# Four VectorE passes instead of five to decode float64 weights, a second slot for magnitudes, and local values in 64-row tiles

## The chip, the cores and the metric

One NeuronCore of a Trainium2 chip runs the whole program. The metric is the device time of one execution in microseconds (us). Three runs of the kernel before took 944.45 to 945.38 us, median 944.99.

## The reference

Three stages follow one another, all in float32 results:

- Attention on q, k, v of shape (4, 8, 576, 64). Two outputs are added: a pooled one (q, k, v averaged in groups of four tokens, softmax over 144 positions, repeated four times) and a local one (each token sees only tokens less than four away, softmax, times v). The heads are laid side by side to x with 2304 tokens of 512.
- A gated layer: `(x @ w_a) * (x @ w_b) @ w_out`, with 512 to 1536 to 512.
- A second layer: `h = x @ w_in; (h * clip(h + 3, 0, 6) / 6) @ w_out`, with 512 to 2048 to 512.

The weights arrive as float64. What the kernel must do with them before any matmul is to turn 64-bit words into 32-bit ones.

## The kernel before, in words

**Precision.** Large matmuls take each operand as two float32r parts (a rounded value and the rest) and three passes (line 635 for the first layer, 692 for its output, 818 and 943/958 for the second layer, whose 2x2 blocks are combined by a seven-product scheme).

**Decoding.** `decode` (line 239) makes a float32 from each float64, 1024 of them on each of 128 partitions, that is one weight tile: 34 tiles in all (12 `wab`, 6 `wo`, 8 `w2i`, 8 `w2o`). A tile is loaded as 8 bytes per weight (line 247) and seen as two uint32 views with a step of two words, `lo` and `hi`. The steps are:

- `magnitude`, ScalarE (256): absolute value of `hi` read as float32, into the tile `m` of tag "dm", of which there is one.
- `exponent`, VectorE (262, 263): clamp, shift left by 3 and mask, in place in `m`.
- `upper`, VectorE (267): the top bits of `hi` joined with `m`, written to `hi`.
- `lower`, VectorE (273, 274): the power of two of the result into `m`; `lo` times 2^-52 times that.
- `both`, VectorE (280): `hi` + `lo`, written to `hi`.
- For `wab` and `wo` then `first` (ScalarE, 284, the rounded part) and `second` (VectorE, 287, the rest); `w2i` and `w2o` have their own steps behind `both`.

**Attention.** Twenty local units of up to 116 tokens (`local`, line 503) and sixteen pooled groups (`pooled`, 375). In a local unit, two sub-blocks of 58 tokens each look at 64 keys. The probabilities of the two heads of a pair lie after the transpose on partitions 0 to 63 and 64 to 127 of `eT`. The values tile `vz` holds the two heads likewise, with a half of zeros for each, so that the product (line 576) takes all 128 rows of `eT` and writes 64 columns of one PSUM bank, `po`. The zeros are written once by GpSimd (line 348), the values by two DMAs per unit (line 517). The score products (line 529) use tiles of 64 rows and 64 columns, in all four positions, with one PSUM bank for each row half.

**Order.** No engine's order is written by hand. `Plan` (line 57) is a list scheduler: every step has an engine, an estimated duration, a due time `want`, predecessors, and slots that it takes and gives. It plays the steps through in estimated time and issues, on each engine, the ready step that is due first; that fixes the order of each engine's in-order queue, SyncE's DMAs included. So any change of estimates, slots or predecessors gives a new order on every engine. Until the first block of x is ready, a filler (line 186, tile `unread`) puts matmuls of no use on TensorE wherever the plan leaves it idle; `end_fill` ends that.

The first layer's jobs (`job`, 618) begin as soon as x of the first block (units 0 and 1) and `wab` tile 0 are there; attention of later units and the decoding of the other `wab` tiles run beside them, to about 300 us. Then come `wo` and `w2i`, the first layer's output (437 to 580 us) beside the decoding of `w2o`, and the second layer (581 us to the end).

Of the kernel before, what the change touches and what calls it, by code (L numbers as in the profile page):

```python
# [9 lines left out]
F32 = mybir.dt.float32  # L10
F32R = mybir.dt.float32r
BF16 = mybir.dt.bfloat16
U32 = mybir.dt.uint32
AF = mybir.ActivationFunctionType
ALU = mybir.AluOpType
# [3 lines left out]
P = 128  # L19
D = 64  # L20
# [3 lines left out]
KB = 64  # L24
QB = KB - 2 * HALO
# [4 lines left out]
HP = 4  # L30
# [2 lines left out]
XT = 3 * UT  # L33
NC = 512
FILL = 0.4
NB = 384
CUT = 4
BANK = 512
# [108 lines left out]
def fused_kernel(ctx: ExitStack, tc: tile.TileContext, qk, vt, vd, wab, wo, w2i, w2o, mask, out):  # L147
    nc = tc.nc
# [3 lines left out]
    F1 = wab.shape[0]  # L152
    F2 = 2 * w2i.shape[0]
    W = 2 * DM
# [5 lines left out]
    dp = dctx.enter_context(tc.tile_pool(name="dec", bufs=1))  # L160
# [4 lines left out]
    ap = actx.enter_context(tc.tile_pool(name="attn", bufs=1))  # L165
# [17 lines left out]
    def fill():  # L183
        if not unread:
# [4 lines left out]

    plan = Plan()  # L190

    BUFS = {"wh": F1, "raw": 2, "dm": 1, "qk": 4, "vraw": 1, "dqk": 2, "de": 2, "dv": 3, "deT": 2, "od": 2, "e": 2,
            "eT": 2, "xf": 2, "x": 4, "a": 2, "b": 4, "s2": 2, "wo": F1 // 2, "w2": 2, "hg0": 3,
            "hg1": 1, "xo": 3, "q": 8, "ws": 2, "x0": 4, "L": 24, "c": 14}
    plan.cap.update(BUFS)
# [4 lines left out]
    def slot(pool, shape, dtype, tag, name):  # L200
        return pool.tile(shape, dtype, tag=tag, bufs=BUFS[tag], name=name)


    def dve(n):
        return 0.07 + 0.00106 * n

    def dve2(n):
        return 0.1 + 0.00055 * n

    def act(n):  # L210
        return 0.1 + 0.00095 * n
# [9 lines left out]
    def ACT(busy, want, run, after=(), take=(), give=(), slack=0.0):  # L221
        return plan.add("ACT", busy, want, run, after, take, give, ACT_L + slack)

    def DVE(busy, want, run, after=(), take=(), give=(), slack=0.0):
        return plan.add("DVE", busy, want, run, after, take, give, DVE_L + slack)
# [10 lines left out]
    wab_t, wo_t, w2_t = {}, {}, {}  # L236
    pools = {}

    def decode(src, want, put, tag, after=(), ahead=4, slack=1.0, raw=None, step=CUT):

        T = {}

        def load(a, b):
            def run():
                if a == 0:
                    T["raw"] = slot(xp if raw == "x" else dp, [P, CUT, W // CUT], mybir.dt.uint64, raw or "raw", "raw")
                nc.sync.dma_start(T["raw"][:, a:b], src[a:b].rearrange("a p c -> p a c"))
            return run

        def words():  # L250
            w = T["raw"].rearrange("p a c -> p (a c)").bitcast(U32).rearrange("p (n t) -> p n t", t=2)
            return w[:, :, 0], w[:, :, 1]

        def magnitude():
            T["m"] = slot(dp, [P, W], F32, "dm", "m")
            nc.scalar.activation(T["m"], words()[1].bitcast(F32), AF.Abs)  # L256

        def exponent():
            m = T["m"]
            mu = m.bitcast(U32)  # L260

            nc.vector.tensor_scalar(m, m, W_MIN, W_MAX, op0=ALU.max, op1=ALU.min)
            nc.vector.tensor_scalar(mu, mu, 3, 0x3FFFFFF8, op0=ALU.logical_shift_left, op1=ALU.bitwise_and)

        def upper():
            hi = words()[1]
            nc.vector.scalar_tensor_tensor(out=hi, in0=hi, scalar=0xC0000000, in1=T["m"].bitcast(U32),
                                           op0=ALU.bitwise_and, op1=ALU.bitwise_or)

        def lower():  # L270
            m, (lo, hi) = T["m"], words()

            nc.vector.tensor_scalar(m.bitcast(U32), hi, 0xFF800000, None, op0=ALU.bitwise_and)
            nc.vector.scalar_tensor_tensor(out=lo.bitcast(F32), in0=lo, scalar=2.0 ** -52, in1=m,  # L274
                                           op0=ALU.mult, op1=ALU.mult)

        def both():
            lo, hi = words()
            v = hi.bitcast(F32)
            nc.vector.tensor_tensor(v, v, lo.bitcast(F32), op=ALU.add)  # L280

        def first():
            T["w"] = put()
            nc.scalar.activation(T["w"][:, 0], words()[1].bitcast(F32), AF.Copy)

        def second():
            nc.vector.tensor_tensor(T["w"][:, 1], words()[1].bitcast(F32), T["w"][:, 0], op=ALU.subtract)


        i, loads = None, []  # L290
        for a in range(0, CUT, step):
            i = DMA(256 * step, want - ahead, load(a, a + step), [i and issued[i]], take=[] if a else [raw or "raw"])
            loads.append(i)
        i = loads
        i = ACT(act(W), want, magnitude, i, take=["dm"], slack=slack)
        i = DVE(2 * dve2(W), want, exponent, [i])
        i = DVE(dve(W), want, upper, [i])
        i = DVE(dve2(W) + dve(W), want, lower, [i], give=["dm"])
        if put is None:
            return DVE(dve(W), want, both, [i], slack=slack), words  # L300
        i = DVE(dve(W), want, both, [i], slack=slack)
        i = ACT(act(W), want, first, [i, *after], take=[tag], slack=slack)
        return DVE(dve(W), want, second, [i], give=[raw or "raw"])

# [37 lines left out]
        return plan.add("-", 0, want, lambda: None, ends, give=[raw or "raw"])  # L342


    vz = [ap.tile([P, 2, 2, HP, D], F32, name=f"vz{i}") for i in range(2)]
    for t in vz:
        for h in range(2):
            nc.gpsimd.memset(t[64 - 64 * h:128 - 64 * h, h], 0.0)

    def unit_tokens(u):  # L350
        return min(UT, S - u % NU * UT)
# [1 line left out]
    place, sizes = {}, []  # L353
    for m, n in enumerate(BLOCKS):
        sizes.append(0)
        for _ in range(n):
            u = len(place)
# [6 lines left out]
    S_ = {}  # L364
# [8 lines left out]
    def one_bank(name):  # L373
        return slot(ps, [P, BANK], F32, "b", name)
# [131 lines left out]
    def local(u, want, soon):  # L506

        L = {}
        b, j = divmod(u, NU)
        tokens = unit_tokens(u)  # L510
        m, at = place[u]
        v_ = vz[u % len(vz)]

        def load():
            for h in range(2):
                r = slice(64 * h, 64 * h + 64)
                nc.sync.dma_start(v_[r, h], vt[u, r])

        def score():
            sc = L["sc"] = two_banks("sc")  # L520
# [47 lines left out]
        def pv():  # L568
            po_ = one_bank("po")
            L["po"] = po_[:, :HP * UT].rearrange("d (p t) -> d p t", p=HP)  # L570
            if soon:
                nc.tensor.matmul(L["po"].rearrange("p a (s r) -> p a s r", r=FACTOR), ident, pooled_part(), start=True, stop=False)
            for p in range(HP):
                for i in range(2):
                    for h in range(2):
                        nc.tensor.matmul(L["po"][64 * h:64 * h + 64, p, i * QB:(i + 1) * QB], v_[:, h, i, p],  # L576
                                         L["eT"][:, p, i * KB:i * KB + QB], start=not soon,
                                         stop=(not soon or (p == HP - 1 and i == 1)))
            if soon:
                L["xf"] = L["po"]  # L580
# [18 lines left out]
        def x_second():  # L599
# [5 lines left out]
        i = PE(0.9, want, score, [S_["sums" if last else "qk", b, g] for g in range(HP)], take=["s2"],  # L605
               give=["qk" if b else "wh"] * HP if last else [])
        S_["score", u] = i
        i = DVE(dve(n) + 0.2, want, top, [i], give=[])
        for p in range(HP):
            i = ACT(2 * 0.31, want, exps(p), [i], take=[] if p else ["e"], give=["s2"] if p == HP - 1 else [])  # L610
        i = DVE(0.36, want, inverse, [i])
        i = DVE(dve(n), want, norm, [i])
        i = PE(0.5, want, turn, [i], take=["b", "turn", "eT"], give=["e"])
        i = ACT(act(n), want, turned, [i], give=["b", "turn"])
        ods_ = [S_["od", b, g] for g in range(HP)]
        i = S_["pv", u] = PE(1.7 if soon else 0.9, want, pv, [i, ld] + ods_,
                             take=["b", "pv"] + ([] if soon else ["xf"]), give=["eT"])
        if not soon:
            i = DVE(dve(n), want, total, [i], give=["b", "pv"] + (["od"] if last else []))
        i = ACT(act(n), want, x_first, [i, S_.get(("x", u - 1)) if at else None], take=[] if at else ["x"])  # L620
# [405 lines left out]
    for u in place:  # L1026
        m = place[u][0]
        i = (place[u][1] + UT - 1) // UT
        t = when[m, 0] - 4 + 0.1 * i if m < 3 else T1 - 30 + 4 * i if m == 3 else T1 - 14 + 1.25 * (i + 3 * m - 12)
# [8 lines left out]
    i = plan.add("PE", 0.01, -1000, fill, take=["b", "m"])  # L1038
    plan.add("-", 0, -1000, end_fill, [i, *(S_["x", u] for u in place if place[u][0] < 1)], give=["b", "m"])
    for f in range(F1):  # L1040
        S_["wab", f] = decode(wab[f], when[0, f] - 4, lambda f=f: wab_t.setdefault(f, slot(wpool, [P, 2, W], F32R, "wh", "wh")),
                              "wh", ahead=26 if f < 2 else 6, slack=0.0)
    for t, (n, f) in enumerate(jobs):
        job(n, f, t, n == NBLK - 1)

# [17 lines left out]
        pctx.close()  # L1063
        pools["ps"] = ctx.enter_context(tc.tile_pool(name="ps2", bufs=1, space=PSUM, reuse_waits="tile"))

    S_["p2"] = plan.add("-", 0, 0, open_p2, [S_["x2", u] for u in place])
    S_["ps"] = plan.add("-", 0, 0, open_ps, [S_["both", n, f] for n, f in jobs[-2:]])

    for i in range(F1 // 2):
# [91 lines left out]
    for i, (n, h) in enumerate((n, h) for n in ORDER for h in range(2)):  # L1161
# [8 lines left out]
        def second(n=n, h=h):  # L1170
# [3 lines left out]
        j = DMA(512, T4 - 24 + 4 * i, load, [x for k in range(CUT * h, CUT * h + CUT) for x in S_["w_d", k]],  # L1174
                take=["wh" if i < F1 else "w2"])
        j = ACT(act(W), T4 - 4 + 4 * i, first, [j])
# [74 lines left out]
```

## Time and profile before

| what | value |
|---|---|
| median of three runs | 944.99 us (944.45 to 945.38) |
| span of the profiled execution, first to last instruction | 942.6 us |
| granted TensorE clock, mean | 1.000 |
| TensorE busy | 934.3 us, 99% |
| VectorE busy | 756.3 us, 80% |
| ScalarE busy | 457.8 us, 49% |
| GpSimd busy | 5.2 us, 1% |
| q1 (the DMA queue of loads and stores) | 49.5% of 16 engines' span |

The profiled execution's own time is not listed apart from its span; the span lies 2.4 us below the median of the runs, and that difference is used for what lies around it. Busy time counts an engine as at work from an instruction's start to its modelled end; the ends of matmuls overlap, so a busy TensorE can still lose time between starts. The page's second part shows the share by 40 slices, the chain of work shows what released what, and the windows view gives busy time by stretch.

### The profile page before, as it was taken

To read this page: it belongs to the slowest core of one execution; us is meant where nothing else is said; L and a number is where in the kernel's file an instruction comes from. 1 tells how busy PE (TensorE), PEld (TensorE's weight loads), DVE (VectorE), ACT (ScalarE), POOL (GpSimd) and SP (SyncE) were. 2 spreads that over 40 slices of the span, in tenths; PEclk is the share of its full clock that TensorE was granted. 3 is DMA by queue.
4 is the path that set the end of the run, shared out by engine and by line. 5 is a ranking of instruction groups with operands and counts; after the bars stand their busy time and mean duration, and the time that the engine had idled before them with its cause. 6 is when DMAs were issued, how large, how long until landed. Compare 5 with 4: busy or idle time off the path is not lost.

```text
span 942.6 us, 19148 instructions
## 1 busy us (share of the span) xinstructions
PE 934.3 (99%) x7306; PEld 874.4 (93%) x7306; DVE 756.3 (80%) x1376; ACT 457.8 (49%) x1164; POOL 5.2 (1%) x44
## 2 busy tenths in 40 slices
PE   9999999999999999999999999999999999999998
PEld 6678999999889999998888889999999999999998
DVE  4999989824736969586877766999898999897983
ACT  3867534535555324223445445545455574554551
POOL 1000000000000000000000000000000000000000
PEclk9999999999999999999999999999999999999999
DMA  9544763423304444426678887425247881806401
GB/s 273 190 125 139 224 218 120 154 70 120 96 31 137 172 149 135 135 81 196 195 227 246 260 264 230 151 97 190 101 164 259 269 259 52 279 7 206 131 18 51
DMA packets 103789, 151.26 MB, mean 160 GB/s; under 512 B 8848, under 2 KB 72336, under 8 KB 103696
## 3 DMA queue, kind: packets, MB, share of 16 engines
q1 hardware_dynamic: 102976, 148.80, 49.5%
q8 instruction: 57, 0.93, 0.4%
q10 hardware_dynamic: 720, 1.23, 0.4%
q14 instruction: 36, 0.29, 0.1%
HBM read 100.19 MB, written 49.81 MB: 159 GB/s over the span
## 4 chain that ended last, share of the span: by engine, by line
PE 92%; DVE 5%; ACT 1%; DMA 1%; issue 1%; DVEq 0%; ACTq 0%
PE pab L635 33%; PE ph L818 19%; PE oacc L958 15%; PE acc L692 14%; PE po L576 2%; PE dsc L426 2%; PE dpo L476 1%; PE sc L529 1%; DVE in L748 1%; PE pt L562 1%; PE oacc L943 1%; PE unread L186 1%; PE dpt L458 1%; ACT e L546 1%; DVE e L914 1%; DMA h<-h_d 1%
## 5 line engine op out<-in xcount | busy, mean ns | idle before, releaser
L635 PE MATMUL pab<-x,wh 128*128 128x344 f32 (+2 forms) x2016 | 321.9, 317 | 0.4 <-DVE x L600 0.4
L635 PEld LDWEIGHTS pab<-x,wh 128*128 128x128 f32 x2016 | 306.2, 188 | 4.3 <-issue 2.0
L818 PE MATMUL ph<-in,w 128*128 128x384 f32 x1008 | 175.3, 335 | 0.0
L818 PEld LDWEIGHTS ph<-in,w 128*128 128x128 f32 x1008 | 175.1, 188 | 0.0
L958 PE MATMUL oacc<-w2o,in 128*128 128x256 f32 x1440 | 173.4, 283 | 1.4 <-DVE in L748 1.4
L958 PEld LDWEIGHTS oacc<-w2o,in 128*128 128x128 f32 x1440 | 172.8, 191 | 2.0 <-DVE in L748 1.8
L692 PE MATMUL acc<-h,wo 128*128 128x512 f32 (+1 forms) x720 | 150.8, 370 | 1.0 <-DVE h L684 0.7
L692 PEld LDWEIGHTS acc<-h,wo 128*128 128x128 f32 x720 | 125.6, 188 | 26.1 <-DVE h L684 1.8
L834 DVE TENSOR_TENSOR part<-ph,part 128x384 f32<-128x384 f32 x168 | 86.0, 552 | 9.5 <-PE ph L818 8.8
L842 ACT ACTIVATE r<-part,three 128x384 f32<-128x384 f32 x96 | 56.4, 613 | 54.3 <-DVE part L834 51.8
L644 DVE TENSOR_TENSOR a<-a,pab 128x344 f32<-128x344 f32 (+2 forms) x84 | 41.4, 494 | 40.4 <-PE pab L635 29.7
L680 ACT ACTIVATE h<-h 128x512 fp32r<-128x512 f32 (+1 forms) x60 | 35.2, 591 | 78.9 <-DMA h<-h_d 75.9
L641 ACT ACTIVATE a<-pab 128x344 f32<-128x344 f32 (+2 forms) x84 | 36.6, 443 | 75.9 <-PE pab L635 49.5
L745 ACT ACTIVATE in<-gr 128x384 fp32r<-128x384 f32 x96 | 47.5, 521 | 41.3 <-PE oacc L958 28.6
L684 DVE TENSOR_TENSOR h<-h 128x512 fp32r<-128x512 f32 (+1 forms) x60 | 38.0, 636 | 36.8 <-ACT h L680 36.8
L256 ACT ACTIVATE m<-raw 128x1024 f32<-128x1024 f32 x34 | 39.1, 1150 | 45.2 <-DVE raw L274 26.7
L748 DVE TENSOR_TENSOR in<-gr,in 128x384 fp32r<-128x384 f32 x96 | 49.8, 555 | 7.0 <-ACT in L745 6.3
L745 ACT ACTIVATE in<-e 128x384 fp32r<-128x384 f32 x72 | 36.5, 526 | 34.0 <-PE oacc L958 20.7
L546 ACT ACTIVATE e<-sc,mx 128x64 f32<-128x64 f32 x160 | 48.1, 322 | 8.7 <-DVE mx L538 8.0
L845 DVE SCALAR_TENSOR_TENSOR r<-r,part 128x384 f32<-128x384 f32 x96 | 50.6, 553 | 1.1 <-ACT r L842 1.1
L274 DVE SCALAR_TENSOR_TENSOR raw<-raw,m 128x1024 f32<-128x1024 uint32 x34 | 41.7, 1227 | 1.2
L280 DVE TENSOR_TENSOR raw<-raw 128x1024 f32<-128x1024 f32 x34 | 41.4, 1217 | 0.3
(91 smaller groups left out, 928.4 us busy)
## 6 DMA issues: line engine op xcount, KB each, us to landing
g_d<-r SPq DMA_DIRECT2D x96, 192.0 KB, 2.0
gr<-g_d SPq DMA_DIRECT2D x48, 384.0 KB, 5.3
raw<-wab SPq DMA_DIRECT2D x12, 1024.0 KB, 13.7
h<-h_d SPq DMA_DIRECT2D x48, 256.0 KB, 3.0
h_d<-a SPq DMA_DIRECT2D x48, 172.0 KB, 2.3
raw<-w2o SPq DMA_DIRECT2D x32, 256.0 KB, 3.6
w2o<-w_d SPq DMA_DIRECT2D x14, 512.0 KB, 7.1
qk<-qk SPq DMA_DIRECT2D x12, 576.0 KB, 7.5
```

The source lines that it names most:

```text
L274: nc.vector.scalar_tensor_tensor(out=lo.bitcast(F32), in0=lo, scalar=2.0 ** -52, in1=m, op0=ALU.mult, op1=ALU.mult)
L280: nc.vector.tensor_tensor(v, v, lo.bitcast(F32), op=ALU.add)
L546: nc.scalar.activation(L["e"][:, p, h], L["s4"][:, p, h], AF.Exp, bias=L["mx"][:, p, h:h + 1], scale=SCALE, accum_out=L["z"][:, p, h:h + 1])
L635: nc.tensor.matmul(T[k], wab_t[f][:, x, c], xs[n][:, g, y, :nb], start=(g == 0 and i == 0), stop=(g == KC - 1 and i == 2))
L692: nc.tensor.matmul(accs[n][e], wo_t[f // 2][:, x, c], hs[n, f][:, y], start=(f == 0 and i == 0), stop=(f == F1 - 1 and i == 2))
L745: nc.scalar.activation(x[0][:, 0], src(), AF.Copy)
L748: nc.vector.tensor_tensor(x[0][:, 1], src(), x[0][:, 0], op=ALU.subtract)
L818: nc.tensor.matmul(acc[k], t[:, x, g * P:(g + 1) * P], X[k, g][0][:, y], start=(g == 0 and n == 0), stop=(g == 1 and n == 2))
L834: nc.vector.tensor_tensor(s[name], acc[k], s[other], op=ALU.add)
L842: nc.scalar.activation(T["r"], src(), AF.Relu, bias=three)
L845: nc.vector.scalar_tensor_tensor(out=T["r"], in0=T["r"], scalar=6.0, in1=src(), op0=ALU.min, op1=ALU.mult)
L958: nc.tensor.matmul(acc[n][e], X[n, k][0][:, x, e * P:(e + 1) * P], t[:, y], start=(k == 0 and i == 0), stop=(k == K - 1 and i == 2))
```

## The change

`decode` loses `lower`. The low word is scaled by 2^-29 and rounded, as an integer, in its own step `rounded`; on VectorE for the first six `wab` tiles (`EARLY = 6`), on ScalarE for all others. It depends on the load alone. `upper` now writes to `m`, and `both` adds the two integers into `hi`. The magnitude slot is given back after `both`, and odd `wab` tiles use a second slot, "am", in the attention pool. The step that closes the attention pool also waits for all `wab` tiles. `vz` loses its halves of zeros, GpSimd's fills go, one DMA loads a unit's values instead of two, and the product takes 64 rows and 64 columns.

```diff
+EARLY = 6
...
-    BUFS = {"wh": F1, "raw": 2, "dm": 1, "qk": 4, ...
+    BUFS = {"wh": F1, "raw": 2, "dm": 1, "am": 1, "qk": 4, ...
...
-    def decode(src, want, put, tag, after=(), ahead=4, slack=1.0, raw=None, step=CUT):
+    def decode(src, want, put, tag, after=(), ahead=4, slack=1.0, raw=None, step=CUT, tm="dm", early=False):
...
         def magnitude():
-            T["m"] = slot(dp, [P, W], F32, "dm", "m")
+            T["m"] = slot(ap if tm == "am" else dp, [P, W], F32, tm, "m")
             nc.scalar.activation(T["m"], words()[1].bitcast(F32), AF.Abs)
+
+        def rounded():
+            lo = words()[0]
+            if early:
+                nc.vector.tensor_scalar(lo, lo, 2.0 ** -29, None, op0=ALU.mult)
+            else:
+                nc.scalar.activation(lo, lo, AF.Copy, scale=2.0 ** -29)
...
         def upper():
-            hi = words()[1]
-            nc.vector.scalar_tensor_tensor(out=hi, in0=hi, scalar=0xC0000000, in1=T["m"].bitcast(U32),
+            mu = T["m"].bitcast(U32)
+            nc.vector.scalar_tensor_tensor(out=mu, in0=words()[1], scalar=0xC0000000, in1=mu,
                                            op0=ALU.bitwise_and, op1=ALU.bitwise_or)
 
-        def lower():
-            m, (lo, hi) = T["m"], words()
-
-            nc.vector.tensor_scalar(m.bitcast(U32), hi, 0xFF800000, None, op0=ALU.bitwise_and)
-            nc.vector.scalar_tensor_tensor(out=lo.bitcast(F32), in0=lo, scalar=2.0 ** -52, in1=m,
-                                           op0=ALU.mult, op1=ALU.mult)
-
         def both():
             lo, hi = words()
-            v = hi.bitcast(F32)
-            nc.vector.tensor_tensor(v, v, lo.bitcast(F32), op=ALU.add)
+            nc.vector.tensor_tensor(hi, T["m"].bitcast(U32), lo, op=ALU.add)
...
-        i = ACT(act(W), want, magnitude, i, take=["dm"], slack=slack)
-        i = DVE(2 * dve2(W), want, exponent, [i])
+        j = ACT(act(W), want, magnitude, i, take=[tm], slack=slack)
+        r = DVE(dve2(W), want, rounded, i) if early else ACT(act(W), want, rounded, i, slack=slack)
+        i = DVE(2 * dve2(W), want, exponent, [j])
         i = DVE(dve(W), want, upper, [i])
-        i = DVE(dve2(W) + dve(W), want, lower, [i], give=["dm"])
+        i = DVE(dve(W), want, both, [i, r], give=[tm], slack=slack)
...
-    vz = [ap.tile([P, 2, 2, HP, D], F32, name=f"vz{i}") for i in range(2)]
-    for t in vz:
-        for h in range(2):
-            nc.gpsimd.memset(t[64 - 64 * h:128 - 64 * h, h], 0.0)
+    vz = [ap.tile([P, 2, HP, D], F32, name=f"vz{i}") for i in range(2)]
...
-            for h in range(2):
-                r = slice(64 * h, 64 * h + 64)
-                nc.sync.dma_start(v_[r, h], vt[u, r])
+            nc.sync.dma_start(v_, vt[u])
...
                     for h in range(2):
-                        nc.tensor.matmul(L["po"][64 * h:64 * h + 64, p, i * QB:(i + 1) * QB], v_[:, h, i, p],
-                                         L["eT"][:, p, i * KB:i * KB + QB], start=not soon,
+                        r = slice(64 * h, 64 * h + 64)
+                        nc.tensor.matmul(L["po"][r, p, i * QB:(i + 1) * QB], v_[r, i, p],
+                                         L["eT"][r, p, i * KB:i * KB + QB], start=not soon,
...
-                              "wh", ahead=26 if f < 2 else 6, slack=0.0)
+                              "wh", ahead=26 if f < 2 else 6, slack=0.0, tm="am" if f % 2 else "dm", early=f < EARLY)
...
-    S_["p2"] = plan.add("-", 0, 0, open_p2, [S_["x2", u] for u in place])
+    S_["p2"] = plan.add("-", 0, 0, open_p2, [S_["x2", u] for u in place] + [S_["wab", f] for f in range(F1)])
```

## Rows read from the trace of the kernel before

**Rows 1.** The page: span, and busy time of each engine (part 1).
```profile
span 942.6 us, 19148 instructions
PE 934.3 (99%) x7306; PEld 874.4 (93%) x7306; DVE 756.3 (80%) x1376; ACT 457.8 (49%) x1164; POOL 5.2 (1%) x44
```

**Rows 2.** Windows: stretch, length, busy PE, PEld, DVE, ACT, POOL; clock, DMA, GB/s.
```profile
21.00:53.00 32.00, 30.85 (x492) 21.17 (x491) 30.62 (x57) 26.88 (x123) 0.00 (x0) 1.00 0.64 190
53.00:100.00 47.00, 46.58 (x539) 40.78 (x536) 45.28 (x84) 31.26 (x119) 0.00 (x0) 1.00 0.45 137
...
560.00:582.00 22.00, 21.19 (x155) 19.73 (x155) 15.15 (x29) 11.30 (x26) 0.00 (x0) 1.00 0.81 252
...
756.00:800.00 44.00, 42.57 (x351) 42.03 (x350) 44.00 (x90) 26.89 (x53) 0.00 (x0) 1.00 0.48 150
```

**Rows 3.** Windows of the filler's matmuls alone (tile unread): busy PE.
```profile
21.00:40.00 19.00, 6.12 (x23) 1.00 0.71 220
...
40.00:53.00 13.00, 3.05 (x11) 1.00 0.54 146
```

**Rows 4.** Groups by line and form: steps of the decoding; busy us, mean ns of one.
```profile
L274 DVE SCALAR_TENSOR_TENSOR raw<-raw,m 128x1024 f32<-128x1024 uint32 x34 | 41.7, 1227 | 1.2
...
L280 DVE TENSOR_TENSOR raw<-raw 128x1024 f32<-128x1024 f32 x34 | 41.4, 1217 | 0.3
...
L263 DVE TENSOR_SCALAR m<-m 128x1024 uint32<-128x1024 uint32 x34 | 23.6, 694 | 1.2
...
L273 DVE TENSOR_SCALAR m<-raw 128x1024 uint32<-128x1024 uint32 x34 | 23.3, 687 | 0.4
...
L256 ACT ACTIVATE m<-raw 128x1024 f32<-128x1024 f32 x34 | 39.1, 1150 | 45.2 <-DVE raw L274 26.7 <-DMA raw<-w2i 13.8 <-DMA raw<-w2o 2.4
```

**Rows 5.** Timeline of the start: start us, us, engine line [idle before <-releaser].
```profile
21.01 1.13 ACT L256 ACTIVATE m<-raw 128x1024 f32<-128x1024 f32 x1
...
21.79 0.69 DVE L537 TENSOR_REDUCE mx<-sc 128x8 f32<-128x512 f32 x1 [0.62 <-PE sc L529]
...
39.58 1.16 ACT L284 ACTIVATE wh<-raw 128x1024 fp32r<-128x1024 f32 x1 [2.17 <-DVE raw L280]
...
48.84 0.71 PE L426 MATMUL dsc<-dqk 64*72 64x144 f32 x8 [0.45 <-ACT e L546]
...
52.97 1.61 PE L635 MATMUL pab<-x,wh 128*128 128x232 f32 x12
```

**Rows 6.** Chain of waits, 18 to 60 us: start us, us, what.
```profile
26.03 1.23 DVE raw L274
...
44.80 2.95 ACT e L546 x20
```

**Rows 7.** Timeline of one unit's score and value products, and one identity product.
```profile
228.61 0.69 PE L529 MATMUL sc<-qk 64*64 64x64 f32 x32
...
231.31 1.15 PE L576 MATMUL po<-eT,vz 128*64 128x58 f32 x32
...
49.49 1.04 PE L572 MATMUL po<-od,ident 128*128 128x464 f32 x2
```

**Rows 8.** Groups by line and form: the same products, mean ns of one.
```profile
L576 PE MATMUL po<-eT,vz 128*64 128x58 f32 x640 | 22.9, 225 | 0.0
...
L529 PE MATMUL sc<-qk 64*64 64x64 f32 x640 | 14.2, 224 | 0.2 <-issue 0.2
...
L572 PE MATMUL po<-od,ident 128*128 128x464 f32 x14 | 6.9, 575 | 0.0
```

**Rows 9.** Timeline 567 to 570 us: a decode in front of an h part.
```profile
567.51 0.68 DVE L273 TENSOR_SCALAR m<-raw 128x1024 uint32<-128x1024 uint32 x1
...
569.84 8.98 PE L692 MATMUL acc<-h,wo 128*128 128x256 f32 x71 [0.52 <-DVE h L684]
```

**Rows 10.** Waits: engine and line, what for, us in total, times, longest.
```profile
ACT m L256 <- DMA raw<-wab: 1.4, 1, 1.4
```

**Rows 11.** Group: GpSimd's fills of zeros.
```profile
L348 POOL MEMSET vz<- 64x512 f32 x4 | 2.1, 518 | 0.2
```

More of the change, by code (lines that the diff above doesn't have):

```diff
@@ L190, in fused_kernel @@
     plan = Plan()
-    BUFS = {"wh": F1, "raw": 2, "dm": 1, "qk": 4, "vraw": 1, "dqk": 2, "de": 2, "dv": 3, "deT": 2, "od": 2, "e": 2,
+    BUFS = {"wh": F1, "raw": 2, "dm": 1, "am": 1, "qk": 4, "vraw": 1, "dqk": 2, "de": 2, "dv": 3, "deT": 2, "od": 2, "e": 2,
             "eT": 2, "xf": 2, "x": 4, "a": 2, "b": 4, "s2": 2, "wo": F1 // 2, "w2": 2, "hg0": 3,
@@ L294, in decode @@
         i = loads
-        i = ACT(act(W), want, magnitude, i, take=["dm"], slack=slack)
-        i = DVE(2 * dve2(W), want, exponent, [i])
+        j = ACT(act(W), want, magnitude, i, take=[tm], slack=slack)
+        r = DVE(dve2(W), want, rounded, i) if early else ACT(act(W), want, rounded, i, slack=slack)
+        i = DVE(2 * dve2(W), want, exponent, [j])
         i = DVE(dve(W), want, upper, [i])
-        i = DVE(dve2(W) + dve(W), want, lower, [i], give=["dm"])
+        i = DVE(dve(W), want, both, [i, r], give=[tm], slack=slack)
         if put is None:
-            return DVE(dve(W), want, both, [i], slack=slack), words
-        i = DVE(dve(W), want, both, [i], slack=slack)
+            return i, words
         i = ACT(act(W), want, first, [i, *after], take=[tag], slack=slack)
```

## The prediction

> **What bounds the kernel now.** I read the page's first part first: TensorE is busy 934.3 of 942.6 us, VectorE 756.3, ScalarE 457.8 [rows 1]. The reader is to see that only 8 us of TensorE's span are empty, so 61 us taken from VectorE (below) can't come back as 61 us. The windows view comes next, because the mean hides the stretches [rows 2]. From 21 to 53 us TensorE looks full, but 6.12 + 3.05 = 9.17 us of it are the filler's matmuls [rows 3], so here it does not set the pace: VectorE works 30.62 of 32 us and ScalarE 26.88. From 53 us on TensorE is short of only 0.42 us in 47, and VectorE, at 45.28, is nearly full beside it. Later it falls short by 0.81 us at 560 to 582 and by 1.43 us at 756 to 800 [rows 2]. So two kinds of gain are open: an earlier first job of the first layer, now at 52.97 us [rows 5], and small gaps later. The chain of waits confirms the first: before 53 us it passes through the decode's passes, such as the 1.23 us one at 26.03, and through ScalarE's exponentials, 2.95 us from 44.80 [rows 6].
>
> **The decode.** Each of the 34 tiles loses two VectorE passes of 687 and 1227 ns [rows 4], 1.914 us, together 65.1 us. Clamp, shift, join and add stay as many and as wide; that the join now writes to `m` and the add reads integers I cost at nothing, as the one-tensor and two-tensor passes cost the same in the rows whether float or integer, stepped or not (694 against 687, 1227 against 1217) [rows 4]. The first six tiles gain one pass on VectorE that reads and writes the stepped low words. No row has a one-tensor pass with a stepped target. The bounds are 0.69 us (such a pass with a stepped source, or in place) and 1.22 us (the add with its stepped target) [rows 4]; I take 0.69, being the same kind of instruction, so these tiles save 1.914 - 0.69 = 1.22 us each (0.69 by the other bound). VectorE is relieved of 65.1 - 6 x 0.69 = 61 us. ScalarE gains 28 passes; the row with stepped source and whole target says 1.15 us [rows 4], 32 us in all.
>
> **Where that lies on the path: the start.** Tiles 0 and 1 are decoded before 53 us. On VectorE that is 2 x 1.22 = 2.44 us, and if the plan puts the first rounding into the 0.62 us for which VectorE waits before 21.79 [rows 5], 3.06 us. That is the upper bound, and the filler's 9.17 us have room for it. The lower bound is 0: ScalarE, with 26.88 of 32 us, is next. The bank whose release starts TensorE at 48.84 is given back by an exponential that ends a solid row on ScalarE [rows 5, 6], and there a free VectorE helps nothing. But ScalarE itself stood for 2.17 us before 39.58 because tile 1's add was late [rows 5], and that wait shrinks with VectorE's work. I take the middle, 1.5 us.
>
> **After the start.** From 53 to 100 us the most that can come is TensorE's 0.42 us [rows 2]; I take 0.3. At 567.51 a pass that goes lies, with its longer partner, in front of an h part for which TensorE stands 0.52 us [rows 9]: 0.5 us. The gaps at 756 to 800 come behind the last decode, and VectorE is full there (44.00 of 44) with other work [rows 2]: 0. ScalarE's 28 passes are covered by its idle time, 16 of 47 us at 53 to 100 and 10.7 of 22 at 560 to 582 [rows 2]. If the cover is gone, one pass delays an h part by 1.15 us, which is the upper end of the cost.
>
> **The value products.** The page shows 640 instructions of 58 columns [rows 8]. One unit's 32 take 1.15 us; less the last one's 225 ns, that is 0.925 us between first and last start, 29 ns each or 0.50 ns per column [rows 7, 8]. The identity product on all 128 rows and columns steps by (1.04 - 0.575) us / 464 = 1.0 ns per column, and the score products, (0.69 - 0.224) us / 32 = 14.6 ns per 64 columns, by 0.23 [rows 7, 8]. I read these as one, two and four tiles at work at a time: 128 x 128, two of 128 x 64, four of 64 x 64. The change uses only two of the four 64 x 64 positions (rows 0 to 63 with columns 0 to 63, and the other diagonal), so still two at a time: 0.925 us as before, 0 gain. The bounds are the score products' step, 0.47 us less per unit, and no overlap, 0.93 us more per unit. The score products keep each row half to its own PSUM bank; the new ones write one bank from both halves, and no row shows that. The Trainium skill speaks against the change here: PSUM — Partial Sum Buffer, section "PSUM bank collisions raise a hardware error", says that row tiles must not use one PSUM bank at the same time, though it reports the error only where they also share a quadrant of 32 partitions. By its strict form the pairs would have to run one after another. The diagonal tiles share no partition, and I keep 0.
>
> **The rest.** One load of 256 KB instead of two of 128 per unit, and GpSimd's four fills of 0.52 us [rows 11] gone: 0. GpSimd is busy 1% [rows 1], and SyncE only loses 20 issues. The wait for all `wab` tiles at the closing of the attention pool: 0, as the last units' x come long after these. The second slot lets a magnitude begin earlier; it is part of the range of the start.
>
> **The sum.** 1.5 + 0.3 + 0.5 = 2.3 us. The profiled span goes from 942.6 to 940.3; with the 2.4 us by which the runs' median lies above the span, 942.7 us against 944.99, or 0.24% less.
>
> **The rivals.**
> - *The gain is given back.* All orders are planned anew. ScalarE sets the start, or the gaps at 560 to 582 and 756 to 800 (0.81 and 1.43 us [rows 2]) double for some other late step. For it: ScalarE at 84% of the start, and a full VectorE at 756. Against it: no later stretch gets more VectorE work. Start 0 to -2 us, gaps +1 to +2: about 944.9 us.
> - *The two row halves take turns on the one bank.* Place: line 576. Price: 20 x 0.93 = 18.6 us, all on TensorE, of which little is idle after 53 us; 963 us. It decides as soon as the pairs' starts are 29 ns apart instead of together. For it: the score products were given two banks. Against it: no shared partitions.
> - *The value products run like the score products.* If the 58 ns per pair came from 128-row weights and not from having two tiles, they gain up to 20 x 0.46 = 9.2 us: 933.5 us after the other gains. The Trainium skill's TensorEngine Tiling, section "Overview", promises up to twice the speed for a contraction of 64 or less. Against it here: the halves of zeros already kept two column tiles busy.
> - *VectorE waits for weights.* The rounding needs only the load, and VectorE's queue is in order: the attention steps behind it, then ScalarE, then TensorE would wait. So far ScalarE took that wait, 1.4 us, once [rows 10]. If four of the six early tiles wait so, TensorE loses up to 5.6 us: 948 us. Against it: ScalarE's first magnitude, at 21.01, waited for nothing [rows 5].
>
> **How the numbers follow.** About 0.2%, 1.9 us, is what a measurement of this kernel can tell from no change; faster means under 943.1, slower over 946.9. The forecast has a chance of 0.57; its parts run from 0 to 3.06 + 0.42 + 0.81 = 4.3 us, so 940.7 to 945.0, and I count 0.5 of the 0.57 as past 1.9 us. Giving back has 0.27, taking turns 0.05, the quick products 0.05, VectorE's waits 0.06. Faster: 0.50 + 0.05 = 0.55. Slower: 0.05 + 0.06 = 0.11. Same: 0.07 + 0.27 = 0.34. The range runs from 940.2 (the best sum, with half a microsecond for a luckier order) to 946.4 (the lower bound of the gains and one ScalarE pass of 1.15 us uncovered, 946.1, with a little for the order); outside lie the two product rivals and most of VectorE's waits, with tails 0.2.
>
> **What would show it.** Right: the groups of lines 273 and 274 are gone, a rounding group of 6 near 0.69 us stands on VectorE and one of 28 near 1.15 us on ScalarE; VectorE busy near 695 us, ScalarE near 490; less filler between 21 and 53 us, and the first job of the first layer at 51 to 52 us; one unit's 32 value products still near 1.15 us. Wrong: the first job at 53 us or later; value products near 0.7 or 2.1 us; VectorE idle on raw loads; TensorE's idle time at 560 to 582 or at 756 to 800 larger by a microsecond or more.

## The result, and the profile after

The changed kernel takes 951.58 us (median of four runs, 949.3 to 952.31) against 944.8 for the kernel before beside it (944.45 to 945.38): a ratio of 1.0065 [1.0052, 1.0077] (the two medians alone give 1.0072). It is 0.65% slower. The forecast was 942.7 with a range to 946.4, so the sign and the range were both wrong.

The page of the kernel after, its span and part 1, which answers to [rows 1]:

```profile
span 950.0 us, 19078 instructions
PE 936.8 (99%) x7305; PEld 876.4 (92%) x7305; DVE 700.6 (74%) x1314; ACT 485.2 (51%) x1192; POOL 3.2 (0%) x40
```

VectorE lost 55.7 us, ScalarE gained 27.4, and the span grew by 7.4. The groups by line and form of the kernel after, which answer to [rows 4, 8] (busy us, mean ns of one, idle before):

```profile
L276 DVE SCALAR_TENSOR_TENSOR m<-raw,m 128x1024 uint32<-128x1024 uint32 x34 | 41.4, 1218 | 0.5
L282 DVE CUSTOM_DVE_ANT_0 raw<-raw,m 128x2048 uint16<-128x2048 uint16 x34 | 41.3, 1216 | 0.8
L265 ACT ACTIVATE raw<-raw 128x1024 uint32<-128x1024 uint32 x28 | 32.4, 1156 | 16.0 <-DMA raw<-wo 9.2 <-DMA raw<-w2i 3.8 <-DMA raw<-w2o 3.0
L574 PE MATMUL po<-eT,vz 64*64 64x58 f32 x640 | 22.9, 221 | 0.0
L263 DVE TENSOR_SCALAR raw<-raw 128x1024 uint32<-128x1024 uint32 x6 | 4.1, 680 | 0.7 <-DMA raw<-wab 0.7
```

Every instruction costs what the prediction took for it. The two passes of 23.3 and 41.7 us are gone, 4.1 us of rounding came; the difference, 60.9 us, is the forecast's 61. (Part 1 counts neighbouring instructions that overlap once, which may be why its VectorE total fell by less.) So the loss is not in the price of any instruction. (The rows count six VectorE passes of the decode before, lines 262, 263, 267, 273, 274 and 280, and four after, five for the first six tiles; the title's five is one too few.)

Where it lies is seen in the windows view of the kernel after (columns as in [rows 2]):

```profile
21.00:53.00 32.00, 30.33 (x466) 21.26 (x466) 31.33 (x58) 27.40 (x118) 0.00 (x0) 1.00 0.63 204
53.00:100.00 47.00, 47.00 (x521) 41.85 (x519) 42.39 (x77) 32.02 (x111) 0.00 (x0) 1.00 0.41 130
...
118.00:146.00 28.00, 24.52 (x235) 22.37 (x234) 24.18 (x43) 18.29 (x64) 0.64 (x8) 0.88 0.77 251
...
122.00:124.00 2.00, 0.11 (x1) 0.14 (x2) 1.65 (x5) 1.19 (x5) 0.10 (x2) 0.85 0.60 134
124.00:130.00 6.00, 6.00 (x21) 5.65 (x22) 5.37 (x8) 5.70 (x18) 0.00 (x0) 0.50 0.96 308
130.00:132.00 2.00, 2.00 (x30) 1.79 (x31) 0.21 (x1) 0.00 (x0) 0.00 (x0) 0.94 0.99 377
...
434.93:587.78 152.85, 150.81 (x721) 125.51 (x721) 90.09 (x145) 71.64 (x115) 0.00 (x0) 1.00 0.77 237
```

Of the stretches that the prediction watched, 53 to 100 us is full (46.58 before). Its window of 560 to 582 us can't be used for the kernel after, because that work runs 6 to 7 us later there; taken from the first product of the first layer's output to the first of the second layer, TensorE is empty for 2.04 us (152.85 less 150.81) where it was 0.99 before. Most of the loss is in a stretch that the prediction never looked at. From 118 to 146 us TensorE is empty for 3.48 us, and behind the largest stop the granted clock is 0.50, the lower level of 1.2 GHz, while the engine works without a pause. The same stretch of the kernel before, and its stretch of the first layer's output:

```profile
118.00:146.00 28.00, 28.00 (x227) 27.53 (x226) 25.29 (x33) 9.37 (x16) 0.00 (x0) 1.00 0.65 208
...
429.22:580.88 151.66, 150.67 (x722) 125.53 (x721) 111.69 (x175) 65.48 (x111) 0.00 (x0) 1.00 0.78 239
```

The timeline of the kernel after, TensorE's rows of that stretch and the first rows of the stages (start us, us, engine and line, what; in brackets the idle time before it and what ended it):

```profile
51.86 1.61 PE L633 MATMUL pab<-x,wh 128*128 128x232 f32 x12
...
114.06 0.69 PE L526 MATMUL sc<-qk 64*64 64x64 f32 x32
...
114.69 6.00 PE L633 MATMUL pab<-x,wh 128*128 128x348 f32 x36
...
123.89 1.08 PE L559 MATMUL pt<-ident,e 128*128 128x128 f32 x4 [2.35 <-DVE e L367]
124.93 6.46 PE L633 MATMUL pab<-x,wh 128*128 128x348 f32 x24
...
133.89 0.63 PE L559 MATMUL pt<-ident,e 128*128 128x128 f32 x4 [0.79 <-ACT x L595]
134.28 4.08 PE L633 MATMUL pab<-x,wh 128*128 128x348 f32 x24
...
140.91 0.42 PE L457 MATMUL dpt<-ident,de 72*72 72x72 f32 x4 [0.35 <-DVE de L367]
...
434.93 8.34 PE L690 MATMUL acc<-h,wo 128*128 128x512 f32 x36
443.84 0.50 PE L690 MATMUL acc<-h,wo 128*128 128x512 f32 x1 [0.58 <-ACT h L678]
...
584.50 3.45 PE L690 MATMUL acc<-h,wo 128*128 128x256 f32 x24 [1.09 <-ACT h L678]
...
587.78 4.50 PE L816 MATMUL ph<-in,w 128*128 128x384 f32 x25
```

And four rows of the same view of the kernel before, which tell when the same work ran there:

```profile
86.06 0.69 PE L529 MATMUL sc<-qk 64*64 64x64 f32 x32
...
107.38 0.60 PE L562 MATMUL pt<-ident,e 128*128 128x128 f32 x4
...
429.22 8.57 PE L692 MATMUL acc<-h,wo 128*128 128x512 f32 x37
...
580.88 11.43 PE L818 MATMUL ph<-in,w 128*128 128x384 f32 x65
```

Read together: the first job starts 1.11 us earlier than before [rows 5], the first layer's output (`acc`) 5.71 us later, the second layer (`ph`) 6.90 us later, and the span ends 7.4 us later. The largest part, 1.11 + 5.71 = 6.8 us, is lost between 53 and 430 us. Another 1.19 us goes in the output itself, 1.05 of it as TensorE's empty time; its two largest stops, 0.58 and 1.09 us, wait for ScalarE's `h`. The reader should also see the order: unit 8's scores ran at 86 us before and 21 us ahead of their transposes; now they run at 114.06 and their transposes stand 9.8 us behind them, so VectorE's softmax (`e` L367) is late for them.

**Why the plan ran into this.** Each first-layer job makes two products; ScalarE copies the first out of PSUM into a tile of tag "a" (`one`, line 639), VectorE multiplies the second into it (`both`, 642), SyncE stores it (645) and the tile is free. There are two such tiles. The timeline of the kernel after, ScalarE, VectorE and SyncE at these lines:

```profile
112.03 0.81 ACT L639 ACTIVATE a<-pab 128x348 f32<-128x348 f32 x2 [1.24 <-PE pab L633]
...
146.23 0.51 DVE L642 TENSOR_TENSOR a<-a,pab 128x344 f32<-128x344 f32 x1
...
117.46 0.33 SPq L645 DMA_DIRECT2D h_d<-a  x1
126.43 0.33 SPq L645 DMA_DIRECT2D h_d<-a  x1
135.07 0.34 SPq L645 DMA_DIRECT2D h_d<-a  x1
```

At 112.03 ScalarE copies two first products, one of them 344 wide (the row is merged and names the other's width): job 16's, of block 1. Its second product carries a later due time than the jobs of block 2, which become ready just then, so the new order puts them in between, and the 344-wide tile is multiplied only at 146.23, 34 us later. Meanwhile all other jobs share one tile and go one by one, with stores at 117.46, 126.43 and 135.07. Their PSUM banks are given back as slowly; as its rules read, the plan then finds nothing else for TensorE and moves unit 8's and unit 9's attention into the hole, just ahead of the work that needs it.

### The profile page after: what moved, and what is told of

The parts are those of the page before. It is cut to its first block, busy times and chain, and to the rows that moved or that the text cites. A ratio compares the mean times of both kernels' runs of the same rounds, so it can differ in the third digit from the quotient of the medians.

```text
span 950.0 us, 19078 instructions
## 1 busy us (share of the span) xinstructions
PE 936.8 (99%) x7305; PEld 876.4 (92%) x7305; DVE 700.6 (74%) x1314; ACT 485.2 (51%) x1192; POOL 3.2 (0%) x40
## 4 chain that ended last, share of the span: by engine, by line
PE 89%; DVE 8%; DMA 1%; ACT 1%; issue 1%; SPq 0%; ACTq 0%; DVEq 0%
PE pab L633 32%; PE ph L816 18%; PE oacc L956 15%; PE acc L690 14%; PE po L574 2%; PE dsc L425 1%; DVE in L746 1%; DMA h<-h_d 1%; PE pt L559 1%; PE sc L526 1%; PE oacc L941 1%; PE dpo L475 1%; PE unread L187 1%; PE dpt L457 1%; DVE e L912 1%; DVE dqk L415 1%
## 5 line engine op out<-in xcount | busy, mean ns | idle before, releaser
L678 ACT ACTIVATE h<-h 128x512 fp32r<-128x512 f32 (+1 forms) x60 | 35.0, 589 | 75.0 <-DMA h<-h_d 60.9
L743 ACT ACTIVATE in<-e 128x384 fp32r<-128x384 f32 x72 | 36.5, 526 | 33.8 <-PE oacc L956 20.8
L282 DVE CUSTOM_DVE_ANT_0 raw<-raw,m 128x2048 uint16<-128x2048 uint16 x34 | 41.3, 1216 | 0.8
L276 DVE SCALAR_TENSOR_TENSOR m<-raw,m 128x1024 uint32<-128x1024 uint32 x34 | 41.4, 1218 | 0.5
```

The costliest lines, as they stand in the source:

```text
L276: nc.vector.scalar_tensor_tensor(out=mu, in0=words()[1], scalar=0xC0000000, in1=mu, op0=ALU.bitwise_and, op1=ALU.bitwise_or)
L743: nc.scalar.activation(x[0][:, 0], src(), AF.Copy)
```

## The experiments

The theory: the instructions are as cheap as forecast, and the loss comes from the new order, in which job 16 holds one of two slots; the stops that follow cost time themselves and lower the clock. The rivals: the new value products cost something; ScalarE's 28 roundings delay the attention; the second magnitude slot brings the disorder; the new instructions cost more in place than in their own rows. The kernel before beside these runs took 944.6 to 945.11 us (medians).

**The values alone.** The kernel before with the change to `vz`, its load and the value products, and nothing else; TensorE's order is that of before.

```diff
-    vz = [ap.tile([P, 2, 2, HP, D], F32, name=f"vz{i}") for i in range(2)]
+    vz = [ap.tile([P, 2, HP, D], F32, name=f"vz{i}") for i in range(2)]
...
-                        nc.tensor.matmul(L["po"][64 * h:64 * h + 64, p, i * QB:(i + 1) * QB], v_[:, h, i, p],
-                                         L["eT"][:, p, i * KB:i * KB + QB], start=not soon,
+                        r = slice(64 * h, 64 * h + 64)
+                        nc.tensor.matmul(L["po"][r, p, i * QB:(i + 1) * QB], v_[r, i, p],
+                                         L["eT"][r, p, i * KB:i * KB + QB], start=not soon,
```

> The kernel before with the local values alone changed (64-row tiles, one load, no fills of zeros); the decode and every engine's order are those of before, but for one load in place of two. Theory, the new order costs the time: 944 to 945.5 us, one unit's 32 value products in 1.15 us. Rival, the two row halves take turns on one bank: 1.15 us becomes about 2.1 and the time 960 us or more. Rival, the product gains from 64 rows: 0.7 us and 936 us.

Measured: 944.94 us (944.12 to 946.18), ratio 1.0 [0.9991, 1.0009]. One unit's 32 value products in its timeline:

```profile
231.26 1.14 PE L572 MATMUL po<-eT,vz 64*64 64x58 f32 x32
```

1.14 us against 1.15 [rows 7]. The values neither gain nor cost.

**The new decoding in the old order.** The kernel before with the values' change and with `upper` and `both` of the change, the rounding on VectorE for all 34 tiles, but planned with before's steps, estimates and slots; TensorE's and ScalarE's orders are those of before.

```diff
         def lower():
-            m, (lo, hi) = T["m"], words()
...
+            lo, hi = words()
+            nc.vector.tensor_scalar(lo, lo, 2.0 ** -29, None, op0=ALU.mult)
+            nc.vector.tensor_tensor(hi, T["m"].bitcast(U32), lo, op=ALU.add)
```

> All new instructions of the decode (the rounding on VectorE for all 34 tiles) and the new values, but planned with the estimates, steps and slots of before, so that each engine keeps the order of before. Theory, the new order costs the time and the instructions are cheaper: VectorE busy 715 us (34 x 1.22 less), no stop of TensorE near 120 us, clock 1.00, time 942 to 944.5 us. Rival, the integer add, the stepped rounding or the values cost the 6 us: 948 us or more in the old order too.

Measured: 944.53 us (943.93 to 945.8), ratio 0.9994 [0.9985, 1.0003]; VectorE busy 719.1 us, clock 1.00. The first job starts at 51.98, 1.0 us earlier. Of that, two thirds are lost again in one wait in front of the first layer's output, which starts 0.36 us earlier than before:

```profile
428.86 16.50 PE L684 MATMUL acc<-h,wo 128*128 128x512 f32 x71 [0.66 <-DVE a L636]
```

The wait is for a multiply into "a" (line 636 there); what makes it late was not tested. The instructions do no harm in place, and 37 us less of VectorE's time give, in the old order, 0.5 us, which the interval does not tell from nothing.

**The old decoding in the new order.** The opposite: the changed kernel's plan, TensorE's and SyncE's orders as there, with before's arithmetic in the steps.

```diff
         def rounded():
-            lo = words()[0]
-            if early:
-                nc.vector.tensor_scalar(lo, lo, 2.0 ** -29, None, op0=ALU.mult)
-            else:
-                nc.scalar.activation(lo, lo, AF.Copy, scale=2.0 ** -29)
+            pass
```

> The reverse of the run with the old order: the old arithmetic of the decode (seven passes, all on VectorE but the magnitude; the rounding's step issues nothing), planned with the estimates, steps and slots of the changed kernel, so that TensorE's and SyncE's orders are those of the changed kernel. Theory, the order costs the time: TensorE stops near 120 us here too and its clock falls, 950 to 954 us. Rival, the new instructions cost the time: 944 to 946 us.

Measured: 968.47 us (967.08 to 970.36), ratio 1.0253 [1.0235, 1.0271], above the 950 to 954 expected. The stop is the same one, and larger; its row in the timeline:

```profile
131.71 1.09 PE L559 MATMUL pt<-ident,e 128*128 128x128 f32 x4 [5.50 <-DVE e L367]
```

It is not the only loss: the first job starts at 55.76 us and the first layer's output at 450.93. With the two kernels this makes a square: old order 945.0 with the old and 944.53 with the new instructions (there with all roundings on VectorE), new order 968.47 and 951.58. The order costs 7 us with the cheap decoding and 23 with the dear one. It was made for a VectorE with 61 us less to do; here VectorE is later than that, and the stop is 5.50 us instead of 2.35.

**One magnitude slot.** The changed kernel without the second slot's use.

```diff
-                              "wh", ahead=26 if f < 2 else 6, slack=0.0, tm="am" if f % 2 else "dm", early=f < EARLY)
+                              "wh", ahead=26 if f < 2 else 6, slack=0.0, tm="dm", early=f < EARLY)
```

> The changed kernel with one magnitude slot for all tiles, as before. Theory, the time hangs on the planned order and not on one part: yet another order, in which unit 8's transposes again stand two steps behind its scores on TensorE, so a stop near 120 us and 946 to 952 us. Rival, the second slot alone turned the order: no stop above 1 us between 100 and 150 us and 943 to 945 us.

Measured: 949.34 us (948.63 to 949.63), ratio 1.0043 [1.0029, 1.0057]. Between 121 and 140 us TensorE has seven stops instead of one large one (the longest 0.78 us). Its window:

```profile
118.00:146.00 28.00, 24.04 (x263) 20.83 (x253) 27.45 (x49) 21.89 (x80) 0.62 (x8) 1.00 0.64 206
```

3.96 us empty, at full clock. The second slot is not the cause, since the hole stays without it. And here too a tile of tag "a" is held, this time by a job of block 0, for 36 us:

```profile
108.66 0.36 ACT L639 ACTIVATE a<-pab 128x232 f32<-128x232 f32 x1 [1.80 <-PE pab L633]
...
144.78 0.39 DVE L642 TENSOR_TENSOR a<-a,pab 128x232 f32<-128x232 f32 x1
```

**Twelve roundings on VectorE.** The changed kernel with none of the first layer's input weights (`wab`) rounded on ScalarE.

```diff
-EARLY = 6
+EARLY = 12
```

> The changed kernel with the rounding on VectorE for all twelve tiles of the first layer instead of six. Theory: the same instructions' work but for six passes moved off ScalarE, another order with unit 8's scores and transposes close together, 946 to 952 us. Rival, ScalarE's roundings of tiles 6 to 11 delay the exponentials and make the stop: it goes, 943 to 945 us.

Measured: 948.66 us (948.4 to 950.13), ratio 1.0042 [1.0026, 1.0057]. The hole is there again; its window shows 4.26 us empty at full clock:

```profile
118.00:146.00 28.00, 23.74 (x265) 21.28 (x264) 26.80 (x43) 14.83 (x48) 0.64 (x8) 1.00 0.80 244
```

The largest of its stops, in the timeline, stands at the transposes of the next unit, 9; the other two rows show that a job of block 1 holds its tile of tag "a" for 34 us here:

```profile
110.92 0.46 ACT L639 ACTIVATE a<-pab 128x344 f32<-128x344 f32 x1 [2.87 <-PE pab L633]
...
131.44 0.66 PE L559 MATMUL pt<-ident,e 128*128 128x128 f32 x4 [1.67 <-DVE e L367]
...
144.59 0.50 DVE L642 TENSOR_TENSOR a<-a,pab 128x344 f32<-128x344 f32 x1
```

ScalarE's roundings of these tiles are not the cause either.

**One job's second product earlier.** The changed kernel with one number of the plan changed: job 16's second product is due 13.5 steps earlier, so that its tile comes free before block 2's jobs.

```diff
-        j = PE(busy, want + 0.5, products(1), [i], take=["b", "m"],
+        j = PE(busy, want + (-13 if want == 16 else 0.5), products(1), [i], take=["b", "m"],
```

> The changed kernel with the due time of one step altered: the second product of job 16, which lay unfinished from 112 to 146 us and held one of the two slots of tag a, becomes due 13.5 steps earlier. Theory, that held slot is what stops TensorE at 121.5 us and lets its clock fall: no stop above 1 us there, clock 1.00, time 943 to 946 us. Rival, VectorE and ScalarE are simply too late with unit 8's exponentials there: the stop stays, 950 us or more.

Measured: 942.95 us (942.39 to 945.06), ratio 0.9979 [0.997, 0.9988]. It beats both kernels. Its window:

```profile
118.00:146.00 28.00, 28.00 (x238) 27.41 (x237) 23.25 (x35) 14.90 (x39) 0.64 (x8) 1.00 0.79 250
```

Its timeline:

```profile
115.34 15.53 PE L633 MATMUL pab<-x,wh 128*128 128x348 f32 x96
...
114.64 0.51 DVE L642 TENSOR_TENSOR a<-a,pab 128x344 f32<-128x344 f32 x1
...
124.39 2.20 SPq L645 DMA_DIRECT2D h_d<-a  x2
...
428.33 16.85 PE L690 MATMUL acc<-h,wo 128*128 128x512 f32 x73
```

Job 16's tile is multiplied at 114.64 instead of 146.23, stores go two at a time (124.39), TensorE is full, and the first layer's output starts 6.6 us before that of the changed kernel and 0.89 before that of the kernel before. The due time of one product takes back the whole loss.

**The same product later.** The other direction, 9.5 steps later than in the change.

```diff
+        j = PE(busy, want + (10 if want == 16 else 0.5), products(1), [i], take=["b", "m"],
```

> The changed kernel with the second product of job 16 due 9.5 steps later still, the reverse of the run that pulled it forward. Theory, the held slot of tag a is what starves TensorE: the slot is held beyond 146 us, further stops of TensorE stand behind 146 us, 952.5 to 956 us. Rival, the stop comes from unit 8's exponentials alone: 951 to 952 us as the changed kernel.

Measured: 955.12 us (954.61 to 958.61), ratio 1.0121 [1.0095, 1.0146]. The first stops are the same (2.35, 0.79, 0.35 us), and new ones follow until 176 us; the tile is multiplied at 165.7. Two rows of its timeline and one window:

```profile
125.42 5.17 PE L633 MATMUL pab<-x,wh 128*128 128x348 f32 x24
...
171.75 2.55 PE L633 MATMUL pab<-x,wh 128*128 128x232 f32 x12 [1.32 <-ACT a L639]
...
172.00:174.00 2.00, 2.00 (x12) 2.00 (x12) 1.54 (x3) 0.00 (x0) 0.00 (x0) 0.54 0.00 0
```

The stop at 171.75 waits for the copy into "a" itself, and the clock falls a second time behind it. More holding, more loss.

**All second products earlier, and a smaller dose.** Two kernels: every second product due 6 ahead of its job's time; and 4 ahead with `EARLY = 4`.

```diff
+        j = PE(busy, want - 6, products(1), [i], take=["b", "m"],
```

> The changed kernel with the second product of every job of the first layer due 6 steps before the first instead of half a step behind it, so that no job lies half done. Theory: no slot of tag a held for long, no stop above 1 us between 100 and 150 us, 942 to 945 us. Rival, half-done jobs are harmless: a stop as in the changed kernel, 948 us or more.

> The changed kernel with four early tiles instead of six, and the second product of every job due 4 steps before the first. Theory: as the run with 6 steps, without a stop, 941.5 to 944 us, that is under both kernels. Rival: 948 us or more.

Measured: 943.55 us (942.2 to 944.44), ratio 0.9984 [0.9975, 0.9993], and 944.15 (943.25 to 945.5), ratio 0.999 [0.9982, 0.9999]. Neither has a stop of TensorE between 118 and 146 us. The general form of the remedy works too, a little less well than the single one; the second kernel lies just above the 941.5 to 944 expected of it.

**The stop filled.** To separate the empty time from the clock: ten matmuls of no use in front of unit 8's transposes, where TensorE stands.

```diff
+            if u == 8:
+                for _ in range(10):
+                    nc.tensor.matmul(pt, idle, idle.unsqueeze(1).to_broadcast([P, BANK // P, P]), start=True, stop=True)
```

> The changed kernel with ten of the filler's matmuls put on TensorE in front of unit 8's transposes, where it stands for 2.35 us at 121.5 us; they write the bank that the transposes write next. Theory, the fall of the clock behind the stop costs as much as the stop: clock 1.00 throughout, the stop's 2.35 us remain as matmuls of no use, and about 3 us come back, 948 to 949 us. Rival, the clock's fall is hidden by waits for other engines: 951 to 952 us.

Measured: 949.69 us (949.29 to 950.84), ratio 1.005 [1.0036, 1.0064], 1.9 us less than the change, where some 3 were expected. Its timeline (its lines stand three further down than the change's):

```profile
121.67 2.33 PE L560 MATMUL pt<-idle 128*128 128x512 bf16 x10
...
125.13 4.09 PE L636 MATMUL pab<-x,wh 128*128 128x348 f32 x24 [0.41 <-ACT a L642]
...
432.70 8.71 PE L693 MATMUL acc<-h,wo 128*128 128x512 f32 x37
```

One of its windows:

```profile
126.00:128.00 2.00, 2.00 (x15) 2.00 (x14) 2.00 (x4) 2.00 (x10) 0.00 (x0) 1.00 1.00 370
```

The clock stays at 1.00, and the 24 products take 4.09 us instead of 6.46. In exchange, the next copy into "a" is now what is late (0.41). The output starts 2.23 us earlier than in the change: that is the clock's net share.

**Over all twelve kernels.** They have eight orders, since three share that of before and three that of the change. From the start of the copy to the end of the multiply, the longest holding of a tile of tag "a" is 5.8 to 11.6 us in the six kernels whose TensorE has no stop above 0.25 us between 100 and 180 us (before, the values alone, the old order, job 16 earlier, and the two with all products earlier). It is 32 to 53 us in the six that have such stops (the change 34.3, one slot 36.5, twelve roundings 34.2, the old decoding 35.2, the stop filled 32.0, job 16 later 53.3). So the long holding goes with the stops in every order that was tried, and moving the held job's due time removes or lengthens both. Each such move is planned anew, though, so other steps move with it.

## Why the prediction was wrong, step by step

**Right in their size.** The decoding's terms (60.9 of 61 us of VectorE's groups). The two-tensor passes: 1218 and 1216 ns, as whole-number passes and with the new target, "at nothing" as taken; the stepped rounding 680 ns, at the bound chosen of 690 and 1220; ScalarE's 1156. The start: 1.5 us taken between 0 and 3.06, measured 1.11 in the change, 1.0 in the old order, 0.45 in the best kernel. VectorE, though, is still the fuller engine there, 31.33 of 32 us, and not ScalarE with 27.40. 53 to 100 us: 0.42 us came back, of which 0.3 was forecast. The values: 0 forecast, 0.0 measured (944.94 against 945.0). The strict rule of the Trainium skill, PSUM — Partial Sum Buffer, section "PSUM bank collisions raise a hardware error", would have had the two diagonal tiles take turns on their bank; the measurement decides against it here, 1.14 us for 32. ScalarE's passes were covered, as said: moving six of them to VectorE leaves the hole where it is, and with all 28 in place it goes when job 16 is moved. The prediction's 963 us for taking turns is the price without the other gains (944.99 + 18.6); from its own 942.7 it would be 961.3, which changes nothing here.

**Wrong in a term.** The 0.5 us at 567.51 did not come: the pass is gone from in front of `h`, but in the same stage TensorE is now empty for 2.04 us instead of 0.99, with a stop of 1.09 us for a later `h`. No run tested what makes that `h` late.

**The step that failed** is in the rival *The gain is given back*: "All orders are planned anew", priced at "gaps +1 to +2", with "no later stretch gets more VectorE work" against it. The sum itself puts the new order at nothing. Two errors stand in the rival. The price was bounded by the gaps that the old order has, 0.81 and 1.43 us; a new order has gaps of its own, and this one has 3.48 us at 118 to 146, where the old order had none. And the argument against it looked at VectorE's load, while what ran short was a tile of tag "a". The working of that rival gives a time near before's, so it could not turn slower, and the two rivals on the slower side had the wrong mechanism: taking turns (963 us) is refuted by the values alone, and in place of VectorE waiting for weights (948 us) there is one wait of 0.7 us in front of all six `rounded` on VectorE.

**The loss, summed from rows.** Against the kernel with one due time moved, the changed kernel is 0.65 us ahead at 115 us (114.69 and 115.34) and 6.60 behind at the first layer's output: 7.25 us. Three stops give 2.35 + 0.79 + 0.35 = 3.49; 24 products at the low clock 6.46 - 4.08 = 2.38; the four transposes 1.08 - 0.63 = 0.45. Together 6.3; the last microsecond was not followed row by row. Behind 430 us the output waits for `h` (0.58 us at 443.84 and 1.09 at 584.50); with job 16 earlier TensorE is empty for 0.33 us in that stage instead of 2.04, and with job 16 later for 0.46, so the held tile does not explain these waits, and their cause stays open. That the plan itself moves the attention because the banks come free late is read from its rules and these rows, not measured by a run of its own. A third tile of tag "a" would test the slot most directly; it was not tried.

**The sum that was meant** comes out nearly whole once the order is mended: 945.0 - 942.95 = 2.05 us, forecast 2.3. That the totals agree is partly luck, as the parts differ: 0.45 us at the start (1.5 forecast) and 0.42 at 53 to 100 make the 0.89 by which the output begins earlier; in the output TensorE is empty for 0.33 us instead of 0.99. The profiled spans differ by 1.4 us (941.2 against 942.6); the rest of the 2.05 lies between these two executions and the medians.

## What to carry to other kernels

Where a planner orders the work, a change of estimates is a change of every queue. Price it by what its scarcest slot can cost, not by the gaps of the old order, and give that a rival on the slower side. Compare a stage over the same work and not over the same microseconds, as the work moves. In the new trace look first for a stretch that was full before and is not now, then for a tile that is held over a long time between two of its steps: here 34 us, for a tile of which there are two. Before a slower version is given up, move single due times: 0.65% slower became 0.21% faster by one number.

## What was unexpected of the hardware

- A stop of 2.35 us was followed by a granted clock of 0.50 (1.2 GHz) for some 6 us in which TensorE worked without a pause, and 24 products took 6.46 us instead of 4.08. Its price isn't fixed: behind the same stop of 2.35 us in the kernel that holds the tile longer the 24 products took 5.17. Nor does the length of one stop decide: in that kernel the clock fell again behind stops of 0.56 and 1.32 us (0.54 from 172 to 174 us). Stops of 1.67 us (twelve roundings) and seven of 0.26 to 0.78 (one slot) left the clock at 1.00, and so did the 2.35 us when it was filled. The Trainium skill's TensorE: Matmul & The Clock Gate, section "What's actually happening", says that there are two levels, that the lower is the default and that activity releases the upper one; the trace agrees, with 1.00 and 0.50 as its levels and 1.00 kept where the stop was filled.
- The add of two tiles of 32-bit whole numbers appears as one custom VectorE instruction on 2048 halves of 16 bits per partition, 1216 ns, as much as the float32 add of 1024 that it replaces (1217 [rows 4]).
